# Another table of offsets for a planner that writes out the instruction order by hand

## The chip, the cores and the metric

The kernel runs on one core of one Trainium2 chip. The metric is the time of one execution on the device in microseconds.

## The reference

Two blocks are applied twice, one after the other, to 2048 tokens of 640 features in bf16: x += A(layernorm(x)), then x += B(layernorm(x)).

```
A: q, k, v = x @ wq, x @ wk, x @ wv          32 heads of 20, 4 segments of 512 tokens
   for each segment s:
     p     = softmax(q k^T * scale + causal mask)
     a_dot = p v
     a_mem = (phi(q) M) / (phi(q) z + 1e-6)  phi(t) = t + 1 if t > 0 else exp(t)
     o_s   = g * a_mem + (1 - g) * a_dot     g = sigmoid(beta), by head
     M    += phi(k)^T v ;  z += sum of phi(k)
   return o @ wo
B: relu(x @ w1) @ w2                         640 -> 1728 -> 640
```

## The kernel before

The work is done by segments: two passes (`a` = 0, 1) of four segments (`s` = 0 to 3), eight in all, each of four token tiles of 128. A segment needs the memory M of the one before it in its pass, and a segment of the second pass needs the rows of x that the first pass has written; so attention, the projections of the next segment and the dense block of an earlier one can run beside each other.

For one segment: LayerNorm on VectorE and GpSimd (`lnorm`, lines 791 to 837), a transposing DMA to the feature layout (`turn`, L813), the projections on TensorE (`group`, L770 and L773), a copy of q and k to DRAM (`spill`, L1066) and back into `pad` with the heads on partitions (`fill`, L1113), the scores (`scores`, L1297, row tiles of 20 partitions), the exponentials on ScalarE (`exps`, L1361), the causal masks on GpSimd (`causal`, L1373), the weighted sums (`apply`, L1393, column tiles), their copy to `otu` (L1403), a transposing DMA to `otk` (`turn_pair`), the division (`divide`, L1479 to L1487), the read of the memory (`mem_read`, L1176 to L1191) and its update (`mem_write`, L1234 to L1261), the sum of both (`combine`, L1506), a transposing DMA to `oT` (`turn_o`), the output projection and residual (`out_proj`, L1515), LayerNorm again, and the dense block (`ffn`, `ffn_rest`, L1568 to L1610).

No loop order is written down. Each of these steps is a Python generator, a stream, added to a planner (`Sched`) in a fixed order: 0 scores, 1 exponentials, 2 masks, 3 weighted sums, 4 free_v, 5 turn_pair, 6 divide, 7 turn_o, 8 and 9 the two halves of the output projection, 10 and 11 the two halves of LayerNorm for the dense block, 12 fill, 13 spill, 14 combine, 15 and 16 phi of k and q, 17 and 18 mem_read, 19 turn_k, 20 mem_write, 21 to 26 and 28 the start of the first segment, 27 LayerNorm for the projections, 29 and 30 the projections of k and q, 31 that of v, 32 and 33 the dense block, 34 the stores, 35 the warm-up products of TensorE, 36 constants, 37 and 38 the loads. A stream yields one operation at a time, with its engine, its planned length, the operations it waits for and the slot (buffer or PSUM bank) that it takes. The planner keeps a planned clock for each engine and again and again records one operation of one stream; what it records is the program, in order on each engine, with the waits that this order needs. It is run when the kernel is built and knows nothing of the run itself.

Which stream is served next is decided in `run` by the smallest key. The planned start is rounded and two things are added to it: a lateness that keeps operations from being recorded close behind a transfer or another engine's result, and an offset from the table `SHIFT`:

```
key = (round(start + late + SHIFT.get(self.place(n, st[1]), 0)),
       0.5 if op.urgent else prio, self.rank[id(st[1])], n)
...
def place(self, n, gen):
    k = self.made.get(id(gen), 0)
    return n, self.phase.get(id(gen), 0), sum(k >= x for x in (6, 20, 60))
```

So an entry `(n, phase, part): ns` moves stream number n in one of its eight phases (one for each segment), in one part of that phase: its first 6 operations, the next 14, the next 40, or the rest. A negative offset lets the stream go ahead of others that could start earlier, a positive one holds it back. Only the pick is shifted; the planned times are not.

Two more rules of the planner matter here. Products can be recorded whole (128 columns of weights, L770) or as four column tiles of 32 (L773); `_mode` records them in the form in which the array stands, or ahead of a weighted sum in quarters, and counts 96 ns for each change of the form. And the scores are recorded two halves at a time, when two of the slots `X`, `Y` (and `Z`, two banks lent to them during the first segment) are free.

All DMAs but a few are issued by SyncE, in recorded order.

Of the kernel before, what the change touches and what calls it, by code (L numbers as in the profile page):

```python
# [159 lines left out]
class Spawn:  # L160
# [12 lines left out]
PE_MARGIN = 80.0  # L173
HOLDERS = 1
SHIFT = {
# [40 lines left out]
}  # L216
HOLD_TOL = {"pe": 220.0, "act": 150.0, "dve": 200.0, "pool": 0.0, "sp": 0.0}

# [1522 lines left out]
```

## Time and profile before

| | us |
|---|---|
| median of three runs | 554.18 (552.16 to 554.33) |
| the profiled execution | 553.16 |
| its span, from the first to the last instruction | 550.7 |
| TensorE busy (98%) | 542.5 |
| VectorE busy (77%) | 426.4 |
| ScalarE busy (74%) | 409.2 |
| GpSimd busy (35%) | 192.5 |

The profiled execution's time is the device's own; the span leaves out what lies around the program's instructions. Busy time counts an engine as busy while any of its instructions runs. Matmuls are pipelined and their ends are modelled, so a TensorE that is busy all the time may still have short waits between two products; start times tell more than the busy share.

### The profile page before, as it was taken

The numbers are of one execution on the slowest core, as the hardware profiler recorded it, in microseconds if no ns is written. First come the engines' busy times: TensorE is split into PE (matmuls) and PEld (weight loads), VectorE is DVE, ScalarE is ACT, GpSimd is POOL, SyncE is SP. The second block draws the span as 40 slices with busy tenths as digits, with TensorE's granted clock in tenths as the row PEclk, the third lists the DMA queues.
The fourth block names the chain that finished last, engine by engine and source line by source line (L and its number), as shares of the span: only waits on it lengthen the run. The fifth ranks groups of instructions, "written<-read, shape, count | busy, mean of one in ns | idle before, by whom it ended". The sixth has DMA issues, their size and how long they took to land.

```text
span 550.7 us, 20357 instructions
## 1 busy us (share of the span) xinstructions
PE 542.5 (98%) x8958; PEld 304.3 (55%) x8958; DVE 426.4 (77%) x1056; ACT 409.2 (74%) x527; POOL 192.5 (35%) x305
## 2 busy tenths in 40 slices
PE   8999999999999999999999999999999999999998
PEld 7443454455554546545556554564645645757656
DVE  5999999798987889897968887886699776836302
ACT  6699899888898997787888878888778877141140
POOL 5255444343443334443433433434134343100000
PEclk9999999999999999999999999999999999999999
DMA  8699997726457172548465624833256411513201
GB/s 272 164 205 261 243 185 187 215 50 108 90 130 129 21 175 82 92 70 118 68 172 109 116 21 133 146 69 69 62 145 116 109 34 21 108 33 56 75 2 51
DMA packets 133323, 62.18 MB, mean 113 GB/s; under 512 B 112116, under 2 KB 123124, under 8 KB 133236
## 3 DMA queue, kind: packets, MB, share of 16 engines
q1 hardware_dynamic: 132672, 60.36, 51.0%
q8 instruction: 70, 1.15, 0.8%
q10 hardware_dynamic: 564, 0.53, 0.4%
q14 instruction: 17, 0.14, 0.1%
HBM read 20.56 MB, written 12.85 MB: 61 GB/s over the span
## 4 chain that ended last, share of the span: by engine, by line
PE 80%; DVE 12%; DMA 4%; SPq 1%; ACT 1%; POOL 1%; issue 0%
PE ps L773 33%; PE ps L770 30%; PE ps L1297 7%; PE ps L1393 6%; DVE stats L791 2%; DVE xn_tok L837 2%; PE ps L1176 2%; DMA x_sb<-in_A_x_dram 1%; DMA oT<-o_sb 1%; DVE o_sb L1487 1%; DVE otu L1403 1%; DMA otk<-otu 1%; DVE w_r L977 1%; PE ps L1234 1%; ACT PT L1361 1%; DMA scr<-stg 1%
## 5 line engine op out<-in xcount | busy, mean ns | idle before, releaser
L1361 ACT ACTIVATE PT<-ps 128x1024 bf16<-128x1024 f32 x320 | 308.7, 1027 | 54.0 <-PE ps L1297 52.4
L1373 POOL TENSOR_SCALAR_AFFINE_SELECT PT<-PT 128x512 bf16<-128x512 bf16 x256 | 166.1, 667 | 240.8 <-ACT PT L1361 240.6
L773 PE MATMUL ps<-xnT,w_r 128*32 128x512 bf16 x1332 | 80.0, 379 | 0.0
L773 PE MATMUL ps<-w_r,hT 128*32 128x320 bf16 (+1 forms) x1796 | 69.3, 295 | 0.0
L1297 PE MATMUL ps<-pad 20*128 20x512 bf16 (+3 forms) x1024 | 63.4, 301 | 0.7 <-ACT PT L1361 0.7
L770 PE MATMUL ps<-w_r,hT 128*128 128x320 bf16 x396 | 63.7, 300 | 0.0
L1610 DVE TENSOR_TENSOR x_sb<-x_sb,ps 128x320 bf16<-128x320 bf16 (+1 forms) x65 | 30.7, 474 | 35.5 <-PE ps L773 30.9
L791 DVE BATCH_NORM_STATS2 stats<-x_sb 128x6 f32<-128x320 bf16 x124 | 54.6, 476 | 4.1 <-DMA x_sb<-in_A_x_dram 3.1
L1591 ACT ACTIVATE hT<-ps 128x512 bf16<-128x512 f32 x47 | 28.1, 599 | 35.4 <-PE ps L773 35.0
L773 PEld LDWEIGHTS ps<-w_r,hT 128*32 128x32 bf16 x1796 | 45.0, 97 | 13.2 <-issue 1.1
L773 PEld LDWEIGHTS ps<-xnT,w_r 128*32 128x32 bf16 x1332 | 32.9, 97 | 30.9 <-issue 3.5
L1590 DVE TENSOR_SCALAR hT<-ps 128x512 bf16<-128x512 f32 x57 | 38.8, 683 | 13.7 <-PE ps L773 11.5
L1297 PEld LDWEIGHTS ps<-pad 20*128 20x128 bf16 x1024 | 17.8, 92 | 52.9 <-ACT PT L1361 26.0
L770 PEld LDWEIGHTS ps<-w_r,hT 128*128 128x128 bf16 x396 | 36.6, 98 | 18.7 <-issue 5.5
L807 POOL TENSOR_TENSOR rstd<-lnU,mhalf 128x2 f32<-128x2 f32 (+2 forms) x27 | 21.0, 779 | 72.2 <-DVE lnU L803 70.7
L770 PE MATMUL ps<-xnT,w_r 128*128 128x512 bf16 x187 | 45.7, 380 | 0.0
L1393 PE MATMUL ps<-PT,v_aug 128*21 128x128 bf16 (+3 forms) x896 | 40.4, 300 | 0.0
L1515 DVE TENSOR_TENSOR x_sb<-x_sb,ps 128x320 bf16<-128x320 bf16 x64 | 29.7, 474 | 11.4 <-PE ps L773 7.4
L1403 DVE CAST otu<-ps 128x512 bf16<-128x512 f32 x46 | 31.5, 684 | 7.4 <-PE ps L1393 7.0
L1487 DVE TENSOR_TENSOR o_sb<-otk,rden 128x320 bf16<-128x320 bf16 x62 | 33.7, 572 | 0.5
L837 DVE TENSOR_SCALAR xn_tok<-x_sb,mv,rstd 128x640 bf16<-128x640 bf16 x60 | 31.1, 552 | 3.4 <-POOL rstd L807 3.3
L1142 ACT ACTIVATE stg<-stg 128x512 bf16<-128x512 bf16 x50 | 31.8, 637 | 2.6 <-DVE rtmp L1140 2.6
(116 smaller groups left out, 727.7 us busy)
## 6 DMA issues: line engine op xcount, KB each, us to landing
pad<-scr SPq DMA_DIRECT2D x124, 80.0 KB
scr<-stg SPq DMA_DIRECT2D x34, 256.0 KB, 2.3
out_dram<-x_sb SPq DMA_DIRECT2D x15, 160.0 KB, 2.1
w_r<-in_B_w_dram SPq DMA_DIRECT2D x10, 216.0 KB, 3.8
w_r<-in_B_w_dram SPq DMA_DIRECT2D x13, 160.0 KB, 2.8
x_sb<-in_A_x_dram SPq DMA_DIRECT2D x10, 160.0 KB, 3.1
scr<-w_r SPq DMA_DIRECT2D x5, 256.0 KB, 3.4
wv_r<-in_A_wv_dram SPq DMA_DIRECT2D x1, 800.0 KB, 9.3
```

The source lines that it names most:

```text
L770: return e.matmul(view(dst.ap, b), a, b, start=(k == 0), stop=(k == last))
L773: return e.matmul(view(dst.ap[rows], b), part, b, start=(k == 0), stop=(k == last))
L791: tk = yield dve(320, 1, lambda e, c2=c2: e.bn_stats(stats6[:, t, c2, :], x_sb[:, t, c2 * 320:(c2 + 1) * 320]), xt)
L837: nm = lambda e, bx, t, k: e.tensor_scalar(bx.ap[:, k * D:k * D + D], x_sb[:, t + k, :], mv[:, t + k, 0:1], rstd[:, t + k:t + k + 1], ALU. ...
L1142: te = yield act(512, lambda e, q=q: e.activation(q, q, ACT.Exp), [tr] + p, psum=False)
L1297: fns.append([(lambda e, z=z, j=j, hh=hh, N=N, o=o, sl=sl, q=hh % 2: e.matmul(slot.ap[:, q, o:o + N], sl.ap[32 * hh:32 * hh + DH, z, 0, 12 ...
L1361: tx = yield act(1024, lambda e, dst=dst, src=src: e.activation(dst, src, ACT.Exp, scale=SCALE), sc + pw)
L1373: tm = yield pool(600.0, lambda e, reg=reg: e.affine_select(out=reg, in_=reg, pattern=[[0, 4], [1, 128]], compare_op=ALU.is_ge, fill=0.0, ...
L1393: fns.append((lambda e, OD, j=j, hh=hh: e.matmul(OD.ap[32 * hh:32 * hh + DH + 1, 128 * j:L], VAUG[vx(a, s)][:, j, 4 * g + hh, :], pt.ap[:, ...
L1403: te = yield evac(L, 1, lambda e: e.tensor_copy(dst, OD.ap), lambda e: e.activation(dst, OD.ap, ACT.Copy), [tk] + OTU[0].tks)
L1487: to = yield dve(320, 1, lambda e, z=z, dst=dst: e.tensor_tensor(dst, av[:, z, :, :, 0:DH], rd.ap[:, z].to_broadcast([128, NJ, 4, DH]), AL ...
L1590: th = yield evac(512, 1, lambda e: e.tensor_scalar(hT[:, dc, :], bk.ap[:, :], 0.0, None, ALU.max), lambda e: e.activation(hT[:, dc, :], b ...
```

## The change

The table `SHIFT` is replaced. The new one comes from a longer run of the same search. The streams, their operations, lengths, waits, slots and priorities, and all other constants are the same. The old table has 242 entries, the new one 252; 14 entries are the same in both, and 301 places have another offset than before (a missing entry is 0). The beginning and the end of the diff, with some of the lines that the prediction speaks of:

```
 SHIFT = {
-    (1, 0, 0): -50, (1, 0, 1): -100, (1, 2, 0): 225, (1, 2, 1): 625, (1, 2, 2): 500, (1, 3, 0): 100, (1, 3, 1): -75,
...
-    (5, 1, 0): -175, (5, 2, 0): -1075, (5, 3, 0): -700, (5, 4, 0): -700, (5, 5, 0): 88, (5, 6, 0): -2000,
-    (5, 7, 0): 425, (6, 1, 0): 150, (6, 1, 1): 200, (6, 2, 0): 737, (6, 2, 1): 462, (6, 4, 1): 24, (6, 5, 0): 250,
...
-    (11, 6, 0): 125, (11, 6, 1): -300, (11, 7, 0): -400, (11, 7, 1): -400, (12, 0, 0): -1450, (12, 0, 1): -1325,
-    (12, 1, 0): 150, (12, 1, 1): 762, (12, 3, 0): 1875, (12, 4, 1): -500, (12, 5, 1): 425, (12, 6, 1): -875,
...
+    (1, 0, 0): -100, (1, 0, 1): -99, (1, 0, 2): 1025, (1, 1, 0): 875, (1, 1, 1): -100, (1, 1, 2): 300, (1, 2, 0): -50,
...
+    (3, 5, 0): -100, (3, 5, 1): -388, (3, 6, 0): -250, (3, 7, 0): -63, (5, 1, 0): -400, (5, 2, 0): 700,
+    (5, 5, 0): -400, (5, 7, 0): -400, (6, 1, 0): 512, (6, 1, 1): 500, (6, 2, 0): 500, (6, 2, 1): 526, (6, 3, 0): -475,
...
+    (12, 0, 0): -1512, (12, 0, 1): -1363, (12, 0, 2): -6000, (12, 1, 0): 387, (12, 1, 1): 200, (12, 2, 0): -925,
+    (12, 2, 1): 4588, (12, 3, 0): 4550, (12, 3, 1): -1575, (12, 4, 0): 25, (12, 4, 1): -3000, (12, 5, 1): 1500,
...
+    (37, 0, 0): -200, (37, 0, 1): -513, (38, 0, 0): -412, (38, 0, 1): -500, (38, 0, 2): -187,
 }
```

71 rows, old and new, of the table SHIFT are left out of this document.

## The prediction

> **What bounds the kernel now.** I read the page first.
>
> ```profile
> span 550.7 us, 20357 instructions
> ...
> PE 542.5 (98%) x8958; PEld 304.3 (55%) x8958; DVE 426.4 (77%) x1056; ACT 409.2 (74%) x527; POOL 192.5 (35%) x305
> ...
> PEclk9999999999999999999999999999999999999999
> ...
> L1361 ACT ACTIVATE PT<-ps 128x1024 bf16<-128x1024 f32 x320 | 308.7, 1027 | 54.0 <-PE ps L1297 52.4
> L1373 POOL TENSOR_SCALAR_AFFINE_SELECT PT<-PT 128x512 bf16<-128x512 bf16 x256 | 166.1, 667 | 240.8 <-ACT PT L1361 240.6
> ```
>
> TensorE is busy 542.5 of 550.7 us at the full granted clock in every slice, and the other engines are far from it. A busy TensorE could still be a loosely packed one, so the next view is the timeline of PE, in a stretch without trouble (start, length, what).
>
> ```profile
> 92.02 0.40 PE L1297 MATMUL ps<-pad 20*128 20x512 bf16 x4
> 92.35 2.55 PE L770 MATMUL ps<-xnT,w_r 128*128 128x512 bf16 x11
> 94.83 0.40 PE L1297 MATMUL ps<-pad 20*128 20x384 bf16 x8
> ...
> 98.01 1.67 PE L770 MATMUL ps<-xnT,w_r 128*128 128x512 bf16 x7
> 99.52 0.33 PE L1176 MATMUL ps<-BD,phs 128*128 128x84 bf16 x3
> ```
>
> From start to start, seven products of 512 columns take 99.52 - 98.01 = 1.51 us, 0.216 each. Eleven of them ahead of a group of scores take 94.83 - 92.35 = 2.48, where 11 x 0.216 = 2.37: the step into the scores costs 0.11. The scores, four products side by side, take 92.35 - 92.02 = 0.33 before the next group starts, 0.11 over one product of 512 columns: the step out of them costs as much. So the stream is packed, and what it pays beside the columns is 0.11 us each time the array changes between whole or column tiles and the row tiles of the scores.
>
> The order can hardly change how often that is. The 320 exponentials each empty one half of scores, the halves are recorded two at a time, so there are 160 pairs and some 320 changes, 160 x 2 x 0.11 = 35 us. To put two pairs next to each other four score slots would have to be free, and the planner has two, three while it borrows; the slots come back one exponential, 1.03 us, at a time. The columns streamed are fixed too, since the operations are the same. What the recording order decides is where TensorE waits. The busy time by stage (PE, weight load, VectorE, ScalarE, GpSimd; then the clock, the DMA engines' share and GB/s):
>
> ```profile
> 0.00:60.00 60.00, 55.97 (x686) 30.32 (x687) 50.79 (x130) 49.78 (x74) 30.61 (x59) 1.00 0.91 228
> 60.00:480.00 420.00, 418.11 (x6481) 228.51 (x6485) 351.79 (x866) 343.21 (x426) 160.50 (x245) 1.00 0.52 108
> 480.00:551.00 71.00, 68.38 (x1800) 45.50 (x1790) 23.82 (x62) 16.24 (x28) 1.39 (x2) 1.00 0.18 45
> ```
>
> PE is idle 60 - 55.97 = 4.03 us in the first 60, 420 - 418.11 = 1.89 in the next 420, and 550.7 - 480 - 68.38 = 2.3 in the rest. Who ended these waits (us in total, times, longest):
>
> ```profile
> PE ps L734 <- DVE warm L677: 1.1, 1, 1.1
> PE ps L1297 <- ACT PT L1361: 0.7, 2, 0.4
> PE ps L773 <- DVE otu L1403: 0.5, 1, 0.5
> PE ps L770 <- DVE otu L1403: 0.5, 1, 0.5
> PE ps L770 <- DVE w_r L1032: 0.5, 1, 0.5
> PE ps L770 <- DMA oT<-o_sb: 0.4, 1, 0.4
> PE ps L770 <- DVE xn_tok L849: 0.4, 1, 0.4
> ```
>
> No wait inside the run is above 0.5 us. A wait costs a little more than its idle entry, because the modelled end of the last product covers the beginning of it:
>
> ```profile
> 54.87 0.39 PE L770 MATMUL ps<-hT,wq_r 128*128 128x512 bf16 x1
> 55.76 0.82 PE L770 MATMUL ps<-hT,wq_r 128*128 128x512 bf16 x3 [0.50 <-DVE otu L1403]
> ...
> 133.32 0.60 PE L770 MATMUL ps<-xnT,wq_r 128*128 128x512 bf16 x2
> 134.35 2.89 PE L770 MATMUL ps<-wo_r,oT 128*128 128x320 bf16 x20 [0.42 <-DMA oT<-o_sb]
> ...
> 258.26 0.86 PE L773 MATMUL ps<-wv_r,xnT 128*32 128x320 bf16 x20
> 259.67 0.59 PE L773 MATMUL ps<-wo_r,oT 128*32 128x320 bf16 x12 [0.54 <-DVE otu L1403]
> ```
>
> 55.76 - 54.87 is 0.89 for one product of 0.216: 0.67 lost, where the entry says 0.50. 134.35 - 133.32 = 1.03 for two: 0.60 lost against 0.42. 259.67 - 258.26 = 1.41 for twenty quarter products, five products of 320 columns, by the same rate 0.135 each (an estimate from the 0.216): 0.73 lost against 0.54. So each wait costs about 0.18 more than is listed.
>
> **The change part by part.** The diff replaces one table by another: 242 entries before, 252 after, 14 of them with the same value, and 301 places whose offset differs, spread over all eight phases (28 to 44 in each). An offset in nanoseconds is added to a stream's planned start when the planner picks what it records next. It adds no instruction and moves no operand; it permutes, on all five engines, which ready operation goes first. So the sum has no term for work, only for waits, and I take it stage by stage.
>
> The fixed parts. The warm-up wait of 1.1 us stands ahead of everything, and the 2.3 us after 480 lie behind the last product: the last store is the same instructions in the same dependency. Both stay. Evacuations may go to ScalarE or VectorE by what is free when they are picked, so the split between the two can shift a little; with 77% and 74% busy neither becomes the bound by that, so zero.
>
> The first 60 us. Idle here is 4.03 - 1.1 = 2.9 us. The three waits shown for VectorE (L770 behind L1403, L1032 and L849) fall in this stage; at 0.18 each they hide another 0.5: 3.4 us in all that an order could win, and this is one end. The other is a loss of the same size, as nothing in a table of offsets excludes it. The releaser is VectorE, which is busy 50.79 of the 60 us, ScalarE 49.78: the matmuls wait in turn for evacuations, on two engines that are at 85% and 83%, while the DMA engines are at 0.91. This is the one stretch where the order matters in many places at once, since VectorE has LayerNorm, evacuations and score bookkeeping to choose among. It can't all go, since nine tenths of the transfer time and five sixths of two engines' time are taken. I take half of it: -1.7 us.
>
> 60 to 480 us. Idle 1.89, and the four waits shown for it (scores behind the exponentials twice, oT at 134.35, otu at 259.67) hide 4 x 0.18 = 0.7: 2.6 us. Two of the four come at the turn from one segment to the next, where the chain of waits runs over a transposing DMA (start, length, what):
>
> ```profile
> 252.47 4.74 DMA otk<-otu
> ...
> 258.21 0.80 DVE o_sb L1487 x2
> 259.01 0.61 DVE otu L1403
> ...
> 259.67 0.86 PE ps L773 x20
> ```
>
> The transfer takes 4.74 us, the division of its result and one more evacuation behind it 1.4, and TensorE runs out of other recorded work 0.73 before that. A new order moves each of these places; what it takes away at one turn it may open at another, because how long a transposing DMA takes beside the other transfers is decided on the chip, and the order is written ahead of it. Bounds: -2.6 if none is left, and +3.8 if all seven turns between the eight segments show one like the worse of the two (7 x 0.73 = 5.1 instead of today's 0.60 + 0.73 = 1.3). I take 0, today's rows, which lie between these ends.
>
> GpSimd's order changes too, above all that of the causal masks. They are 0.67 us each, and the engine stands idle 65% of the span waiting for exponentials, so I price that at nothing; a mask that comes behind another operation would hold back the weighted sums by about its own length, and TensorE only where the planner has nothing else recorded.
>
> A rule weighed: the row says 0.11 us for each change of tiling, and a new order could change more often, above all between whole and quartered products. The Trainium skill, TensorEngine Tiling (Array Packing), Key Properties, says that changing the tiling mode drains the array, while another tile in the same mode does not. The trace agrees as far as the scores go, at 0.11 us; by the page the step from whole to quartered products would drain as well, and 16 more of those would eat the 1.7.
>
> The sum: -1.7 + 0 = -1.7 us. The profiled execution took 553.16 us, 2.46 more than its span; the span becomes 549.0 and the execution 551.5. The median of the three runs, 554.18, lies 1.02 above the profiled execution, and by that the median after is 552.5 us.
>
> **The rivals.** First, the packing works at both ends: the first stage gives 2.6 of its 3.4 us and the rest 1.6 of its 2.6. That is 554.18 - 4.2 = 550.0 us. For it: every one of these waits is short, 0.2 to 0.5 listed, and has other ready work near it. Against it: VectorE at 85% in the first stage, and transfers of nearly 5 us at the turns.
>
> Second, slower: SyncE's queue at the turns. SyncE issues in recorded order the refills of pad, the spills, the loads and all transposing DMAs, and it stops at each one's wait. The offsets of the refill stream go from 0 to -6000 in one place of phase 0 and from 0 to +4588 in one of phase 2, those of the transposes of the attention result (turn_pair) from -1075, -700, -700 and -2000 to +700, 0, 0 and 0 in phases 2, 3, 4 and 6. If a transpose is recorded behind a refill or spill whose source isn't ready, it starts late, and behind it stand the division, the residual, LayerNorm and the next segment's projections. As long as TensorE has more recorded work than the transfer and the 1.4 us behind it, nothing shows; from there every microsecond does, in full. The price is the upper bound above, +3.8 us with no gain ahead of it: 558.0 us. For it: the two turns that already show it. Against it: no such wait is now over 0.73 us, and it takes all seven turns.
>
> Third, also slower, with a smaller place: more changes between whole and quartered products, at 0.11 each by the nearest row, that of the scores. From 41 more on, 4.5 us less the 1.7, it decides: 557.0 us.
>
> Fourth, the new table orders the same work as well as the old one and no better: waits come and go, 554.2 us. That many offsets never decide a pick, being added to streams that have nothing else ready beside them, speaks for it.
>
> **How the numbers follow.** Half a per cent of 554.18 is 2.8 us, about what a measurement of this kernel can tell from no change; the three runs of before span 2.2. The forecast, a gain between 0 and 2.8, has 0.34. The fourth rival, between 0 and a loss of 2.8 with its centre near 0, has 0.15. The first, a gain over 2.8, has 0.31: it needs nearly half of the 6.0 us that both stages hold together. The second has 0.16 and the third 0.04. So faster 0.31, same 0.49, slower 0.20. The range goes down to 548.6, the first rival and 1.4 us more, close to the 548.2 that are left when all 6.0 are won, and up to 557.0, which leaves out most of the second rival and half of the third; 0.04 lie below and 0.14 above.
>
> **What would show it.** In the profile after, the score groups should still stand alone, so that PE's busy time stays within a microsecond of 542.5; if it rises by more, the third rival is at work. The idle time of PE in the first 60 us should fall from 4.03 to about 2.5. Between 60 and 480 it should stay near 1.9, with waits for oT or for the division behind otk at one to three turns. A wait of more than 1 us for one of these would show the second rival, and an idle time near 1 us in the 420 together with less than 2 in the first 60 the first. The forecast is wrong if the early idle time does not fall, or if the turns give back more than it gains.

## The result: 0.3% faster, 551.97 us

The median went from 553.42 us (551.37 to 557.46) to 551.97 us (550.25 to 554.09), 22 runs each; the ratio is 0.997, with a 95% interval from 0.9956 to 0.9983. That is 1.4 us by the medians and 1.7 by the ratio. The gain is real and lies within the half per cent that was called no change. The profiled execution took 552.55 us, a little over the median, with a span of 550.5.

The page after, in the lines that answer to those of before:

```profile
span 550.5 us, 21498 instructions
...
PE 541.5 (98%) x9528; PEld 308.1 (56%) x9528; DVE 430.0 (78%) x1066; ACT 404.4 (73%) x517; POOL 195.3 (35%) x305
...
PEclk8999999999999999999999999999999999999999
...
L1362 ACT ACTIVATE PT<-ps 128x1024 bf16<-128x1024 f32 x320 | 308.9, 1039 | 63.1 <-PE ps L1298 61.8
```

There are 570 more matmuls, because more of them are recorded in quarters, four instructions for one product. TensorE is busy a microsecond less. The busy time by stage, and who ended TensorE's waits:

```profile
0.00:60.00 60.00, 55.03 (x644) 31.30 (x644) 48.85 (x129) 48.07 (x72) 30.05 (x57) 0.97 0.89 224
60.00:480.00 420.00, 418.53 (x7132) 230.94 (x7128) 358.41 (x880) 340.08 (x418) 163.72 (x247) 1.00 0.56 108
480.00:551.00 71.00, 67.97 (x1768) 45.86 (x1760) 22.73 (x58) 16.25 (x28) 1.52 (x2) 1.00 0.24 47
```

```profile
PE ps L747 <- DMA beta_z<-in_A_beta_dram: 1.8, 1, 1.8
PE ps L735 <- DVE warm L678: 1.1, 1, 1.1
PE ps L1298 <- ACT PT L1362: 1.0, 4, 0.3
PE ps L771 <- DMA oT<-o_sb: 0.8, 1, 0.8
PE ps L774 <- issue: 0.4, 1, 0.4
PE ps L771 <- DMA wq_r<-in_A_wq_dram: 0.4, 1, 0.4
```

Idle time in the first 60 us did not fall: it is 60 - 55.03 = 4.97 us where it was 4.03. A new wait of 1.8 us leads the list: the small product with beta, which was recorded behind the first transposes, now stands ahead of them and waited for its load. Between 60 and 480 us TensorE is idle 1.47 us instead of 1.89, with one wait of 0.84 for oT at the turn at 256 us, about where the old order waited 0.54 for otu at 259.67.

So the start of this execution is late and its body is short. The first scores and the last product, before and then after:

```profile
19.17 0.39 PE L1297 MATMUL ps<-pad 20*128 20x512 bf16 x4
...
548.14 0.24 PE L773 MATMUL ps<-w_r,hR 128*32 128x160 bf16 x4
```

```profile
20.91 0.39 PE L1298 MATMUL ps<-pad 20*128 20x512 bf16 x4
...
547.73 0.24 PE L774 MATMUL ps<-w_r,hR 128*32 128x160 bf16 x4
```

From the first scores on, the old order took 548.14 - 19.17 = 528.97 us and the new one 547.73 - 20.91 = 526.82: 2.15 less, 1.74 of which this execution had lost ahead of the scores.

What is shorter in the body can be read in one place. The update of the memory M multiplies 128 rows of weights with the columns of all heads that they touch, 147 or 168. Recorded whole, a product streams all of them; recorded in quarters, each quarter of 32 rows streams only the 42 or 63 columns of its own heads, except in the first product of a sum, which must fill the bank. The groups of this line by form, before and after (the shape behind the tiles is that of the array, 128*128 for whole):

```profile
L1234 PE MATMUL ps<-v_aug,phk 128*128 128x147 bf16 x32 | 3.3, 228 | 0.1
...
L1234 PE MATMUL ps<-v_aug,phk 128*32 128x63 bf16 x72 | 2.3, 191 | 0.0
L1234 PE MATMUL ps<-v_aug,phk 128*32 128x42 bf16 x108 | 2.3, 183 | 0.0
...
L1234 PE MATMUL ps<-v_aug,phk 128*32 128x147 bf16 x48 | 1.8, 230 | 0.0
...
L1234 PE MATMUL ps<-v_aug,phk 128*128 128x168 bf16 x8 | 1.7, 233 | 0.0
...
L1234 PE MATMUL ps<-v_aug,phk 128*32 128x168 bf16 x12 | 0.7, 233 | 0.0
L1234 PE MATMUL ps<-w_r,phk 128*128 128x147 bf16 x8 | 0.7, 228 | 0.0
```

```profile
L1235 PE MATMUL ps<-v_aug,phk 128*32 128x63 bf16 x108 | 3.5, 191 | 0.0
L1235 PE MATMUL ps<-v_aug,phk 128*32 128x42 bf16 x160 | 3.4, 183 | 0.0
...
L1235 PE MATMUL ps<-v_aug,phk 128*32 128x147 bf16 x72 | 2.7, 229 | 0.1
...
L1235 PE MATMUL ps<-v_aug,phk 128*32 128x168 bf16 x20 | 1.2, 233 | 0.0
L1235 PE MATMUL ps<-v_aug,phk 128*128 128x147 bf16 x10 | 1.0, 229 | 0.0
...
L1235 PE MATMUL ps<-w_r,phk 128*128 128x147 bf16 x8 | 0.7, 228 | 0.0
```

48 products were whole, 18 are now. Of the 30 that have become quarters, 22 are short (the short quarters in these rows rose from 180 to 268) and 8 are first products that still stream all columns (60 such quarters before, 92 now). Four quarters run side by side, so I count a quarter's columns as a fourth: the rows of v_aug then add up to 10584 columns before and 8337 after, and by this count no other tile's columns differ between the two orders. At 0.216 us for 512, the 2247 columns fewer are 0.95 us, an estimate. What one product costs stands in the timelines, before and after:

```profile
83.43 0.78 PE L1234 MATMUL ps<-v_aug,phk 128*128 128x147 bf16 x9
84.05 0.59 PE L770 MATMUL ps<-hT,wq_r 128*128 128x512 bf16 x2
```

```profile
251.43 0.47 PE L1235 MATMUL ps<-v_aug,phk 128*32 128x147 bf16 x32
251.73 0.71 PE L1569 MATMUL ps<-xnT,w_r 128*32 128x256 bf16 x20
```

Nine whole ones take 84.05 - 83.43 = 0.62 us, 0.069 each; eight quartered ones, two of them first products and six short, take 0.30, 0.0375 each. 30 times the difference is 0.9 us, the same as by the columns; put on the short ones alone, it is 0.04 us each. A second saving of the same kind: in the order of matmuls that the two traces show, the array's form changes 326 times before and 322 times after. The 320 around the scores are the same; the steps from whole products straight to quartered ones, without scores between, fell from six to two. At 0.11 us that is 0.4 us, and 1.3 us with the memory update.

### The profile page after: what moved, and what is told of

It is laid out like the page before. It is cut to its first block, busy times and chain, and to the rows that moved or that the text cites. A ratio compares the mean times of both kernels' runs of the same rounds, so it can differ in the third digit from the quotient of the medians.

```text
span 550.5 us, 21498 instructions
## 1 busy us (share of the span) xinstructions
PE 541.5 (98%) x9528; PEld 308.1 (56%) x9528; DVE 430.0 (78%) x1066; ACT 404.4 (73%) x517; POOL 195.3 (35%) x305
## 4 chain that ended last, share of the span: by engine, by line
PE 87%; ACT 5%; DMA 3%; DVE 3%; POOL 0%; issue 0%; SPq 0%
PE ps L774 37%; PE ps L771 33%; PE ps L1298 8%; PE ps L1394 6%; ACT PT L1362 5%; PE ps L1177 2%; DMA wq_r<-in_A_wq_dram 1%; DMA phk<-phs 1%; DMA oT<-o_sb 1%; DVE hT L1591 1%; PE ps L1235 1%; PE ps L1569 1%; DVE otu L1404 0%; POOL PT L1374 0%; DVE phs L1144 0%; DVE o_sb L1488 0%
## 5 line engine op out<-in xcount | busy, mean ns | idle before, releaser
L1374 POOL TENSOR_SCALAR_AFFINE_SELECT PT<-PT 128x512 bf16<-128x512 bf16 x256 | 168.8, 677 | 250.4 <-ACT PT L1362 250.2
L774 PE MATMUL ps<-xnT,w_r 128*32 128x512 bf16 x1604 | 96.1, 379 | 0.0
L774 PEld LDWEIGHTS ps<-xnT,w_r 128*32 128x32 bf16 x1604 | 40.1, 97 | 37.0 <-issue 3.7
L1592 ACT ACTIVATE hT<-ps 128x512 bf16<-128x512 f32 x51 | 30.4, 599 | 29.1 <-PE ps L774 28.9
L1404 DVE CAST otu<-ps 128x512 bf16<-128x512 f32 x54 | 37.1, 687 | 10.4 <-PE ps L1394 9.4
L1591 DVE TENSOR_SCALAR hT<-ps 128x512 bf16<-128x512 f32 x53 | 36.0, 683 | 6.9 <-PE ps L774 6.2
L1488 DVE TENSOR_TENSOR o_sb<-otk,rden 128x320 bf16<-128x320 bf16 x62 | 36.2, 608 | 1.7 <-DMA oT<-o_sb 1.1
L838 DVE TENSOR_SCALAR xn_tok<-x_sb,mv,rstd 128x640 bf16<-128x640 bf16 x60 | 29.5, 531 | 3.0 <-POOL rstd L808 2.9
L1394 PEld LDWEIGHTS ps<-PT,v_aug 128*21 128x21 bf16 x896 | 20.5, 92 | 19.0 <-POOL PT L1374 2.8
```

The costliest lines, as they stand in the source:

```text
L774: return e.matmul(view(dst.ap[rows], b), part, b, start=(k == 0), stop=(k == last))
L1374: tm = yield pool(600.0, lambda e, reg=reg: e.affine_select(out=reg, in_=reg, pattern=[[0, 4], [1, 128]], compare_op=ALU.is_ge, fill=0.0, ...
L1394: fns.append((lambda e, OD, j=j, hh=hh: e.matmul(OD.ap[32 * hh:32 * hh + DH + 1, 128 * j:L], VAUG[vx(a, s)][:, j, 4 * g + hh, :], pt.ap[:, ...
L1404: te = yield evac(L, 1, lambda e: e.tensor_copy(dst, OD.ap), lambda e: e.activation(dst, OD.ap, ACT.Copy), [tk] + OTU[0].tks)
L1488: to = yield dve(320, 1, lambda e, z=z, dst=dst: e.tensor_tensor(dst, av[:, z, :, :, 0:DH], rd.ap[:, z].to_broadcast([128, NJ, 4, DH]), AL ...
L1591: th = yield evac(512, 1, lambda e: e.tensor_scalar(hT[:, dc, :], bk.ap[:, :], 0.0, None, ALU.max), lambda e: e.activation(hT[:, dc, :], b ...
```

## The experiments

Five questions were open: whether the wait for beta belongs to the new order, whether the memory update is worth what the rows say, where in the run the gain lies, whether a planned wait comes out on the chip, and what a change of form costs.

**The new table again.** No edit. 

> The new table unchanged, on the chip and in the rounds of the next three. Both theories: 0.997 of the old table, about 1.5 us less. Its profile shows whether the 1.8 us that TensorE waited for beta in the first profile after the change is there in every run: theory A (the wait belongs to the new order, since the small product with beta now stands ahead of the first transposes) says a wait of 1 us or more again; theory B (the loads of that one run happened to land late) says under 0.5 us.

551.61 us, ratio 0.9974 (0.9962 to 0.9986). The waits of its profile:

```profile
PE ps L771 <- DVE w_r L1033: 2.1, 1, 2.1
...
PE ps L771 <- DMA wq_r<-in_A_wq_dram: 0.6, 1, 0.6
```

The same program did not wait for beta at all, nor for oT; it waited 0.6 us for wq and then 2.1 us for an evacuation of v. On VectorE this evacuation stands behind a LayerNorm whose rows of x took 9.1 us to land. Theory A falls as far as the 1.8 us go: they belonged to that execution. The start was late again, at 21.36 us, in another place.

**The beta product moved back.** Two numbers: the planner is told that beta lands later, and the stream's offset is dropped.

```
- lat=1470.0 if name[:2] == "x0" else ...
+ lat=4500.0 if name == "beta" else 1470.0 if name[:2] == "x0" else ...
-    ... (35, 0, 0): -5775, ...
```

Apart from two memsets that change places on VectorE, nothing else moves. 

> The new order with one thing moved: the product with beta stands behind the first transposes and the first projection of k again. Theory A: the wait for beta is gone and TensorE starts the first transposes at 5.8 us instead of 7.5, so the time falls by 1.0 to 1.7 us against the new table, to 0.995 of the old one or less. Theory B: the first weights set the head, the time stays within 0.4 us of the new table, 0.997.

551.07 us, ratio 0.9971 (0.995 to 0.9992): no difference from the new table that can be measured, though the interval just reaches theory A's 0.995.

**The beta product put first in the old order.** `yield Need("first", 1)` ahead of it becomes `Need("first", 0)`; nothing else moves. 

> The old order with the product with beta put ahead of the first transposes, nothing else moved. Theory A: TensorE waits for beta as in the new order, 1.0 to 1.8 us more, 1.002 to 1.003 of the old table. Theory B: no difference beyond 0.4 us, 1.000.

553.37 us, ratio 1.0002 (0.9989 to 1.0014). Theory B holds: in the old order the interval excludes theory A's 1.002, and in the new one nothing was won by moving the product. The first loads land at different times from run to run. The larger load of wk took these times (KB, median us from issue to landing), in the profile of the new table, of its second execution, and of the one with beta moved:

```profile
wk_r<-in_A_wk_dram SPq DMA_DIRECT2D x1, 480.0 KB, 8.0
```

```profile
wk_r<-in_A_wk_dram SPq DMA_DIRECT2D x1, 480.0 KB, 7.5
```

```profile
wk_r<-in_A_wk_dram SPq DMA_DIRECT2D x1, 480.0 KB, 6.3
```

The first scores started at 20.91, 21.36 and 18.63 us; with the old table, where the load took 6.8, at 19.17. This load is issued at 2.76 or 2.77 us in all of them. It does not set the start alone: the latest start, 21.36, came with a load of 7.5 us and through the later load of x. In the profile after there is a third cause. From 9.52 to 12.93 us its granted clock was 0.50, and 30 products of 128 columns that took 10.97 - 9.10 = 1.87 us in the second execution took 12.91 - 9.71 = 3.20 there. That is 1.3 of the 1.74 us which this execution had lost ahead of the scores.

**Half old, half new.** The planner is made to follow a recorded list of picks: the old run's up to the pair of scores at 89 us, then the new run's without what has been recorded already; and the reverse. 

> The old order as far as the pair of scores at 89 us, the new order from there on. Theory E (the gain comes from the body, and the new order's first 60 us cost some of it: in three profiles of the new order the first scores started at 20.91, 21.36 and 19.58 us, in two of the old one at 19.17 and 18.70): 1 to 1.5 us less than the new table, 0.995 of the old one, and the first scores at 19.2 us or before. Rival F (the first 60 us vary by run with the landing of the first loads, and both orders do the same there): 0.997, as the new table.

552.35 us, ratio 0.9974 (0.9958 to 0.9989). 

> The reverse: the new order as far as the pair of scores at 89 us, the old order from there on. Theory E: 1 us more than the old table, 1.002, with the first scores at 20 us or later. Rival F: as the old table, 1.000. If instead most of the gain sat in the first 90 us, 0.998 or less.

552.98 us, ratio 0.9987 (0.9972 to 1.0003). Rival F: with the old start and the new rest the whole gain is there; with the new start and the old rest none is left that is clear of 1. In both profiles the first scores were late, at 20.76 and 20.36 us, so a late start is not a mark of either order. As far as the gain is clear, it lies behind 89 us, but the second interval reaches down to 0.9972 and does not exclude that a part lies ahead. The forms of the products say that a part does: the old order has 54 short products in the memory update and the new one 76; the first of these runs has 67 and 322 changes of form, the second 63 and 326. At 0.04 and 0.11 us that is 1.0 us for the first and 0.4 for the second, 0.9982 and 0.9993, both inside the intervals.

**The memory update without its saving.** In the quartered products each quarter takes all columns of the group; the order is the same.

```
- hs = heads_of(c, y) if i else (CH_H0[c], CH_H1[c])
+ hs = (CH_H0[c], CH_H1[c])
```

> The new order; the quartered products of the memory update take all the columns of their group of heads (147 or 168) instead of the 42 or 63 that their 32 rows need; results are the same and the order too. Theory C: the new order gains by recording 30 more of these products in quarters, of which 22 with fewer columns; by the starts in the profiles a whole one takes 0.069 us and four short quarters 0.0375, so 0.03 each, 76 such products here: 2.3 us more than the new table, about 1.001 of the old one, and 22 x 0.03 = 0.7 us is what the change had from it. Rival D (quarters hide behind other work, or their weight loads bind them): within 0.5 us of the new table.

> The old order with the quartered products of the memory update over all columns of their heads, as the new order had them before. Theory C: there are 54 of the short ones here against 76 in the new order; at the 1.8 us that the 76 cost there, 1.3 us more than the old table, 1.0023. The new order in this form was at 1.0007, so that 0.9 us of the gain would be left for fewer changes of form and fewer waits. If the difference between the two tables closes altogether, 1.001 or less here, the memory update was all of it.

The new order in this form took 553.3 us, ratio 1.0007 (0.9992 to 1.0022); the old one 554.37 us, ratio 1.0013 (0.9999 to 1.0028). The saving is on the path, as theory C says: without it the new order gives up 0.33% (1.0007 against 0.9974), 1.8 us, which the two intervals leave uncertain by about 1 us. The place shown above now reads

```profile
251.40 0.70 PE L1235 MATMUL ps<-v_aug,phk 128*32 128x147 bf16 x32
251.93 0.72 PE L1569 MATMUL ps<-xnT,w_r 128*32 128x256 bf16 x20
```

0.53 us for the eight, against 0.30: 0.23 for six short ones, 0.038 each. So 76 short ones are 2.9 us by the rows, not the 2.3 of the expectation, which took all eight for short. With the saving taken from both orders they are 0.0006 apart, not more than their intervals hold, where the tables were 0.003 apart. The old order lost 0.7 us by it instead of the 1.3 expected, within its interval; but by the rows its 54 short products are 2.1 us, and the interval ends at 1.5. So a part of this saving does not reach the time there, and which waits take it up was not tried. The memory update carries a good part of the gain, from 0.9 us by the rows to nearly all of it by these two times; the intervals of about 0.15% do not split it further, nor do they show that nothing else is left.

**More changes of form.** The new order, pick by pick, with 90 products of the dense block behind 480 us recorded whole between quartered neighbours. 

> The new order, operation by operation, with 90 of the 361 products of the dense block behind 480 us recorded whole instead of in quarters, each between quartered neighbours: 180 more changes of the array's form (502 instead of 322), the same columns. The third rival's price, 0.11 us for each change: 19.8 us more than the new table, about 1.033 of the old one. If only the step from whole to quartered products costs, the one direction that the profiles of both tables show: 9.9 us, about 1.015. If only the row tiles of the scores drain the array: 0.997, as the new table.

572.09 us, ratio 1.0323 (1.0297 to 1.035). Against the new table's 0.997 that is 0.0353 x 553.15 = 19.5 us for 180 changes, 0.108 us each.

```profile
529.73 0.83 PE L802 MATMUL ps<-xnT,w_r 128*32 128x512 bf16 x12
530.50 0.39 PE L799 MATMUL ps<-xnT,w_r 128*128 128x512 bf16 x1
530.82 0.83 PE L802 MATMUL ps<-xnT,w_r 128*32 128x512 bf16 x12
```

The single whole product takes 0.32 us to the next start where its columns need 0.216, and the three quartered ones take 0.77 where they need 0.65: it costs about 0.11 in either direction, not only around the scores.

**No table.** `SHIFT = {}`. 

> All offsets left out. The planner's own clock for TensorE ends 9.3 us later than with the old table. Theory G (a wait that the recorded order contains comes out on the chip in full, since TensorE has no slack anywhere): 8 to 11 us more than the old table, 1.015 to 1.020, and the profile's idle time of TensorE rises by as much. Rival H (the engines run ahead of the plan, and most planned waits vanish): under 4 us, below 1.007.

562.73 us, ratio 1.0167 (1.0138 to 1.0195): by the ratio 9.2 us more than the old table's 553.62, where the planner's clock had 9.3. Its longest entry of waits (us in total, times, longest):

```profile
PE ps L1257 <- ACT PT L1321: 5.6, 9, 2.0
```

Theory G, as to the time. The offsets as a whole are worth 1.7%, and they earn it for the most part by keeping TensorE from waiting: for the exponentials ahead of the scores above all, up to 2.0 us at a time. TensorE idles 563.4 - 547.2 = 16.2 us in this profile against 8.2 before, though this execution was the longest of its four. A part is work again: 15 short products in the memory update instead of 54, and 334 changes of form instead of 326, 2.4 us by the rows.

**One stream's new offsets in the old table.** The entries of stream 5 (turn_pair) are those of the new table, the rest is old. 

> The old table with the new table's offsets for one stream alone, the transposes of the attention result: the place of the second rival. The planner's clock ends 2.4 us later than with the old table. Theory G: 2 to 3 us more, 1.004 to 1.0055. The second rival (transposes late in SyncE's queue cost more than planned): over 3.5 us, 1.0065 or more, with waits of TensorE for oT or for the division at most of the seven turns. Rival H: under 1 us.

554.55 us, ratio 1.0014 (1.0001 to 1.0028): 0.8 us more, where the planner's clock had 2.4. The time is that of rival H. But the forms moved here too: 45 short products in the memory update instead of 54, and 327 changes instead of 326, 0.5 of the 0.8 us by the rows. Its profile lists

```profile
PE ps L1296 <- ACT PT L1360: 1.0, 2, 0.6
...
PE ps L772 <- DVE otu L1402: 0.4, 1, 0.4
PE ps L769 <- DMA oT<-o_sb: 0.3, 1, 0.3
```

The wait for the exponentials, 1.0 us in total, was 0.7 before, and the transposes at the turns cost no more than before. By these figures 0.3 us is left for waits, with an interval of 0.1 to 1.5 us for the whole. Why most of the planned wait did not come stays open. The planner's transfers are planned with a fixed latency, and the traces show the transposes landing earlier or later than that; whether this is the reason was not tried.

## Why the prediction was right, and where its steps were not

The number held: 552.5 us was forecast with a gain within half a per cent, and 551.97 us came, by a gain of 0.3%. Its working did not. It counted from 554.18, the median of three runs, where the old table's median over 22 is 553.42. A gain of 1.7 us was forecast from waits of the first 60 us, which did not shrink, and one of much the same size came in the main from work whose change was put at nothing; that the two agree is luck. By the sign that the prediction itself named, that the early idle time falls, its mechanism was wrong.

**The fixed columns.** "The columns streamed are fixed too, since the operations are the same" is the step that failed. The operations are the same, but the planner chooses for each product whether it is recorded whole or in quarters, and in the memory update the quartered form streams fewer columns. The order decides the form, so the order decides some of the work: 0.9 us by the rows, shown to lie on the path by taking it away. The rule for this stood in the code (`heads_of` in the quartered variant, planned at 38 ns a product against 66 whole), and the rows of L1234 in both forms stood in the profile before; the sum had no term for it. The planner's own clock held it too: when the two kernels are built, TensorE's plan ends at 544.89 us with the old table and at 543.60 with the new one. Of these 1.29 us, 1.00 is shorter planned work, 0.62 in the memory update and 0.38 in the changes of form.

**The changes of form.** The price of 0.11 us, taken from the scores, was right for the other changes too (0.108). The scores did stay alone, with 320 changes around them in both orders. The sign for the others was not right: the third rival let the new order change more often, and it changes four times less, 0.4 us. The Trainium skill's rule (TensorEngine Tiling (Array Packing), Key Properties: a change of the tiling mode drains the array) was weighed with the trace agreeing for the scores only; the run with 180 more changes agrees for whole and quartered products as well.

**The first 60 us.** -1.7 us was forecast there, and nothing of it came. The idle time rose from 4.03 to 4.97 in one profile and to 6.67 in the second execution of the same program, and with the new start but the old rest the time was not clear of the old table's. In the very first part the waits depend on the landing of the loads, which changes by more than a microsecond from run to run; what sets the others was not tried. Half of 3.4 us was a choice without a row behind it.

**60 to 480 us.** 0 was forecast for the waits, and 1.47 against 1.89 us of idle time is near enough. The turns behaved as said: one opened (0.84 for oT), another closed (0.54 for otu), and in a second execution of the same program the wait for oT was gone. What the step did not have is the work that fell inside this stretch.

**The rivals.** SyncE's queue did not decide: the longest wait at a turn in the profile after is 0.84 us, and turn_pair's new offsets put into the old table cost 0.8 us, not at the turns, and more than half of it by the rows through the forms. The offsets of the refill stream were not tried alone. The first rival's 4.2 us lie far outside the interval, which ends at a gain of 2.4. The fourth rival, no better and no worse, is excluded by the interval, though only by 0.2%.

The saving by the rows, 0.9 + 0.4 = 1.3 us, leaves 0.1 to 0.4 us of the 1.4 to 1.7, about the fall of idle time in the body, from 1.89 to 1.47. That the fall is the new order's and not the run's is not shown: the same program idles 0.65 us in this stretch in its second execution.

## What to carry to other kernels

Where a planner may record the same product in different forms, a change of order is a change of work: count instructions by form in both profiles before calling the work fixed, and read the planner's own clock for both orders. When the bound engine is packed, the price of its changes of mode (0.11 us here, 320 of them for the scores alone) and the columns of each form are firmer ground for a sum than the waits, of which half a microsecond comes and goes from run to run. And a difference in the first 20 us between two single profiles should be looked for in a second execution of the same program before it is laid to the change.

## What the runs showed of the hardware

A change between whole and quartered products costs as much as one into or out of row tiles, 0.108 us on average over 180. The larger load of wk, issued at the same time, took 6.3 to 8.0 us to land in different profiles; the first scores varied by 2.7 us, through this load, a later one of x and the clock. In the profile after, where TensorE stood 1.8 us for beta at 5.7 us, the granted clock of the first 60 us shows 0.97 (0.50 from 9.52 to 12.93 us), and products of 128 columns that started 0.28 us apart in groups of five (9.10 and 9.38 us in the second execution of the same program) started 0.53 apart:

```profile
9.71 0.74 PE L771 MATMUL ps<-xnT,wk_r 128*128 128x128 bf16 x5
10.24 0.74 PE L771 MATMUL ps<-xnT,wq_r 128*128 128x128 bf16 x5
```

```profile
9.10 0.44 PE L771 MATMUL ps<-xnT,wk_r 128*128 128x128 bf16 x5
9.38 0.44 PE L771 MATMUL ps<-xnT,wq_r 128*128 128x128 bf16 x5
```

The Trainium skill (TensorE: Matmul & The Clock Gate, What's actually happening) says that an idle window lets the array fall back to half its clock. The halved rate agrees with it, the condition does not: the wait is shorter than the window of about 3.4 us that the page gives, and the slow products come 2 us behind its end. Nor does the length of a wait alone decide: in the second execution TensorE waited 2.1 us ahead of 18.79 us, and the granted clock stayed at 1.00. What lowered it here is not shown.
